# Row lists, expert rows, attention's weight pieces and gate weights' sums of a retention, mixture-of-experts and SoLU kernel at other places of its program

## The chip, the cores and the metric

The kernel runs on one core of a Trainium2 chip. The metric is the device time of one execution in microseconds (us). Before the change it is 546.37 us, the median of 3 runs (546.04 to 546.61).

## The reference

Three layers follow one another. The first is a retention (a linear attention with decay) over 2 batches of 768 steps, 8 heads of 64; its output is 1536 tokens of 512 values. The second gives each token to the best two of 8 experts; the gate has added noise. The third is a dense layer with a softmax-weighted activation and a norm.

```
for t in range(S):                                   # retention
    state = gamma * state + einsum('bhd,bhe->bhde', k[:, :, t], v[:, :, t])
    y[:, :, t] = scale * einsum('bhd,bhde->bhe', q[:, :, t], state)

noisy = x @ w_gate + log1p(exp(x @ w_noise)) * noise # experts
top2 = argpartition(-noisy, 2, axis=1)[:, :2]        # softmax of the two gives top2_w
for e in range(8):
    h = maximum(x[mask] @ w1[e], 0)                  # 512 -> 1024
    out[mask] += top2_w[mask, k] * (h @ w2[e])       # 1024 -> 512

h = x @ w_in                                         # 512 -> 1024
solu = h * softmax(h)
out = (layernorm(solu) * g_ln) @ w_out               # 1024 -> 512
```

## The kernel before

**Order.** Nothing reorders the program. Each engine runs its instructions in the order in which the code issues them, and an instruction that has to wait holds up all behind it on its engine or queue. So the order of the Python code is the order of every engine, and generators (`choose`, `slots`, `load_xg`, `convert_steps`) are stepped with `next` where a piece of their work is to stand. Loads and stores are issued by SP (a few by ACT at the start); gathers by index are issued by POOL, as are the first four weight pieces of the second expert.

**Numbers.** A product of float32 values is made of three: each operand is split into a high part (ACT copies it to a rounded type) and a low part (DVE subtracts). So `hidden` issues 12 matmuls for one block of 128 hidden columns, as xh·wh, xh·wl and xl·wh. The names: `wr` a raw piece of weights (512 KB), `wh` and `wl` its parts, `xh` and `xl` those of an expert's input rows, `hh` and `hl` those of the hidden values.

**Attention.** The loop `for i in range(NT)` runs over 12 tiles of 128 tokens. Of a tile PE makes `y_out` (from state and masked scores), `kv` (the state), `scores` of the next tile, and `x_rows` (rows of x and gate logits in one). DVE makes `vp` (for the first five tiles; ACT later), `pm` (masked scores), `xT` and the logits. Beside this stand the gate's steps: `choose(g)` finds the best two experts for a group of tiles, `rank(g)` each token's place in its expert's list, `slots` and `add_table` turn places into a table of token numbers, `by_rows` spreads the table (`spread`). `feed(split_to, load_to, later)` loads raw weight pieces and splits them; here piece i is split at tile i and three more are loaded.

**First expert.** The expert with most tokens has number 0 in w1 and w2 and is done first, in two parts: `hidden(0, f, slice(0, EARLY))` for 192 rows of the first 8 tiles (f from 0 to 7), then the other 256 rows once their list is there: `rank(3)`, `first_rows(3)`, `list_part(1)`, the gather of the rows, and `first_xt(1)`, which transposes them on PE. `turns` sorts the other experts by their number of tokens.

**The seven others.** `lists` makes `rows_r`, the row numbers for all of them. `load_xg(e)` gathers an expert's rows (four tiles by POOL). For expert 1, PE transposes these (`xg_t`, line 995). From expert 2 on they take another path: stored to `xs` in DRAM, read back as `xq` with the columns regrouped, and transposed by DVE in blocks of 32 (line 999). `load_xg` stops after each gather, each pair of stores and each pair of reads. Before the change it is stepped for expert e + 2 within expert e: gathers at f = 4 to 7 (a POOL copy to `pace` holds each back until `hh` of that f is there), stores in the second half, and the reads at f = 1 and 3 of expert e + 1.

An expert e has 8 blocks of `hidden`, in PSUM banks `b` and `a` in turn (two of each), then `second`: four quarters of 24 matmuls into banks `c0` to `c3` (line 1036). `xg_t` of the next expert stands behind the first two quarters. `y_t` transposes the result of the expert before and stores it to `yg`. `advance` calls `feed` and so sets when pieces are split and loaded: a load waits for one of four buffers, which a split sets free. `convert` makes float32 of the last layer's weights, a piece at a time.

**Last layer.** `weights` makes the two gate weights of each token and the rows of `yg` where its two results lie (`slot_y`). The last expert's second product has three blocks of 128 rows (line 1139); behind the first, POOL starts to gather results (`gather`, line 798), `mix` adds a token's two results, `x2_t` transposes, `h_in` multiplies by w_in (line 837), `solu` and `z_turn` make z and turn it by way of DRAM (`zd`, `zc`), `z_parts` splits it, `out_mm` multiplies by w_out (line 924).

Of the kernel before, what the change touches and what calls it, by code (L numbers as in the profile page):

```python
# [44 lines left out]
def retnet_moe_solu(ctx, tc, qT, kT, k, v, w_gate, w_noise, noise, w1, w2, w_in, w_out, g_ln,  # L45
# [442 lines left out]
    def choose(g):  # L488
# [10 lines left out]
        nc.scalar.activation(r, p[:, :, E:2 * E], AF.Relu)  # L499
        V.scalar_tensor_tensor(ab, th, -1.0, th, op0=OP.mult, op1=OP.max)  # L500
        V.tensor_scalar_mul(nl, ab, LOG2[0])
        for n, c in enumerate(LOG2[1:-1]):
            if n == 0:
                yield
            V.scalar_tensor_tensor(nl, nl, c, ab, op0=OP.add, op1=OP.mult)
# [77 lines left out]
    def add_table(lo):  # L583
        oh, nm = HOT.pop(lo)
        last = oh.shape[1] - 1
        p = bank("a", (128, 32))
# [37 lines left out]
    def first_xt(part, d):  # L624

        n = BLKS[2 * part][1]
        p = bank("a", (128, 2, 2 * n)) if n <= 128 else None
# [11 lines left out]
    def turns():  # L639

        V = nc.vector
        p = bank("c2", (128, E))
# [19 lines left out]
    def lists():  # L662

        p = bank("a", (128, E - 1, 4))
# [30 lines left out]
    def hidden(e, f, c):  # L695
# [7 lines left out]
        for n, (w, x, d) in enumerate(terms):  # L703
            nc.tensor.matmul(p, w[:, 0, f * 128:(f + 1) * 128], x[:, d, c],  # L704
                             start=(n == 0), stop=(n == len(terms) - 1))
        nc.scalar.activation(hh[:, f, c], p, AF.Relu)  # L706
# [20 lines left out]
    for i in range(NT):  # L727
# [5 lines left out]
        if i in (4, 8, 10):  # L733
            next(picks)
        if i == 6:
            next(todo, None)
        if i:
            kv(i)
        if i == 5:
            rank(0)  # L740
        if i == 7:
# [5 lines left out]
        if i == NT - 1:  # L747
            rank(2)
            for d in (0, 2):
                first_xt(0, d)  # L750
# [3 lines left out]
        if i in (5, 9):  # L754
            next(picks, None)
        if i == 5:
# [11 lines left out]
        scale_v(i + 2)  # L768
        if i == 9:
            list_part(0, range(4, 8), "a", last=True)  # L770
        if i in (3, 7, 9, 11):
# [3 lines left out]
            next(picks)  # L775
        if i % 2 == 0:
            dec_t(i // 2 + 1)
        feed(min(i, LEAD), min(i + 3, LEAD + 3), later)
# [4 lines left out]
    next(last_picks, None)  # L783
# [152 lines left out]
    hidden_of(0)  # L936
    for f in range(KF):
# [110 lines left out]
    for e in range(E - 1):  # L1048
        if e:
            hidden_of(e)  # L1050
        for j in range(4):
            for f in (2 * j, 2 * j + 1):
# [22 lines left out]
                if f in (1, 3, 4, 5):  # L1075
                    d = (1, 3, 4, 5).index(f)
                    if e:
                        y_t(e - 1, d)
# [255 lines left out]
```

## Time and profile before

| | us |
|---|---|
| median of 3 runs | 546.37 |
| the profiled execution | 547.89 |
| its span, from the first instruction to the last | 545.8 |
| PE busy (matmuls) | 515.7, 94% |
| DVE busy | 369.6, 68% |
| ACT busy | 232.6, 43% |
| POOL busy | 100.1, 18% |
| TensorE's mean granted clock | 0.981 |

PE, DVE, ACT and POOL are TensorE, VectorE, ScalarE and GpSimd; PEld is TensorE's weight load. A busy time is the sum of an engine's own intervals. The profiled execution lies 2.09 us over its span and 1.52 us over the median. The attention takes the first 76 us of the span, the first expert until 135, the others until 402, the last layer the rest.

In the timeline view a row has the start in us, the length in us, the engine, the line, the operation, written and read tiles, shapes, the number of merged instructions, and in brackets the idle time before with what ended it.

### The profile page before, as it was taken

To read this page: it belongs to the slowest core of one execution; us is meant where nothing else is said; L and a number is where in the kernel's file an instruction comes from. 1 tells how busy PE (TensorE), PEld (TensorE's weight loads), DVE (VectorE), ACT (ScalarE), POOL (GpSimd) and SP (SyncE) were. 2 spreads that over 40 slices of the span, in tenths; PEclk is the share of its full clock that TensorE was granted. 3 is DMA by queue.
4 is the path that set the end of the run, shared out by engine and by line. 5 is a ranking of instruction groups with operands and counts; after the bars stand their busy time and mean duration, and the time that the engine had idled before them with its cause. 6 is when DMAs were issued, how large, how long until landed. Compare 5 with 4: busy or idle time off the path is not lost.

```text
span 545.8 us, 8617 instructions
## 1 busy us (share of the span) xinstructions
PE 515.7 (94%) x3059; PEld 469.8 (86%) x3059; DVE 369.6 (68%) x743; ACT 232.6 (43%) x434; POOL 100.1 (18%) x202
## 2 busy tenths in 40 slices
PE   9889988969999899999999979999989999999996
PEld 8878887859999799999999979999768888888886
DVE  5678778728747877857877658867357676676650
ACT  3576732424423343434425234445345445434341
POOL 4000011250020050220310400000333544331110
PEclk9999999979999899999999997999989999999999
DMA  8998431566694897796996986867453565564341
GB/s 247 344 364 309 136 108 40 171 216 222 195 300 159 276 287 266 215 319 193 296 339 199 242 269 217 216 215 171 140 197 90 159 189 175 158 164 139 96 117 44
DMA packets 71857, 111.92 MB, mean 205 GB/s; under 512 B 9760, under 2 KB 37152, under 8 KB 71808
## 3 DMA queue, kind: packets, MB, share of 16 engines
q1 hardware_dynamic: 65520, 94.58, 57.2%
q0 software_dynamic: 4944, 16.39, 9.5%
q8 instruction: 26, 0.43, 0.3%
q10 hardware_dynamic: 1344, 0.34, 0.3%
q14 instruction: 23, 0.19, 0.1%
HBM read 83.50 MB, written 27.79 MB: 204 GB/s over the span
## 4 chain that ended last, share of the span: by engine, by line
PE 41%; DVE 22%; DMA 15%; ACT 6%; issue 5%; SPq 3%; POOL 0%; DVEq 0%; POOLq 0%; ACTq 0%
PE d L837 12%; PE b L924 12%; DVE wl L195 5%; PE a L704 4%; PE c L1036 4%; PE b L704 4%; DMA yg<-yr 3%; DVE xt L999 3%; DMA xs<-xr 3%; ACT xh L1001 2%; DMA wr<-in_moe_w_dram 2%; DVE hl L707 2%; DMA xq<-xs 2%; DVE xl L1002 2%; ACT wh L194 2%
## 5 line engine op out<-in xcount | busy, mean ns | idle before, releaser
L195 DVE TENSOR_TENSOR wl<-wr,wh 128x1024 fp32r<-128x1024 f32 x68 | 81.4, 1219 | 24.1 <-ACT wh L194 24.1
L1036 PE MATMUL c<-hh,wh 128*128 128x448 f32 (+5 forms) x224 | 80.0, 357 | 0.1
L1036 PE MATMUL c<-hl,wh 128*128 128x448 f32 (+5 forms) x224 | 79.6, 355 | 0.0
L1036 PE MATMUL c<-hh,wl 128*128 128x448 f32 (+5 forms) x224 | 79.4, 355 | 0.0
L194 ACT ACTIVATE wh<-wr 128x1024 fp32r<-128x1024 f32 x68 | 69.6, 1050 | 21.3 <-DMA wr<-in_moe_w_dram 21.3
L704 PE MATMUL b<-xh,wh 128*128 128x192 f32 (+8 forms) x144 | 48.1, 342 | 6.4 <-ACT xh L1001 3.4
L704 PE MATMUL b<-xh,wl 128*128 128x192 f32 (+8 forms) x144 | 47.4, 337 | 0.0
L704 PE MATMUL a<-xh,wh 128*128 128x256 f32 (+7 forms) x128 | 44.1, 348 | 1.4 <-DVE table L589 1.3
L1036 PEld LDWEIGHTS c<-hh,wh 128*128 128x128 f32 x224 | 42.7, 191 | 2.0 <-issue 0.7
L704 PE MATMUL a<-xh,wl 128*128 128x256 f32 (+7 forms) x128 | 43.8, 346 | 0.0
L1036 PEld LDWEIGHTS c<-hh,wl 128*128 128x128 f32 x224 | 42.7, 190 | 1.3
L1036 PEld LDWEIGHTS c<-hl,wh 128*128 128x128 f32 x224 | 42.7, 191 | 1.2
L798 POOL DMA_INDIRECT y<-yg,slot_y x24 | 24.7, 1031 | 90.5 <-DMA yg<-y 77.0
L1073 POOL COPY pace<-hh 1x1 f32<-1x1 f32 x20 | 10.0, 498 | 159.0 <-ACT hh L706 158.8
L837 PE MATMUL d<-wh,x2h 128*128 128x512 f32 x96 | 38.9, 405 | 0.0
L924 PE MATMUL b<-wh,zh 128*128 128x512 f32 (+1 forms) x104 | 38.3, 375 | 0.0
L924 PE MATMUL b<-wl,zh 128*128 128x512 f32 (+1 forms) x104 | 38.2, 374 | 0.0
L837 PE MATMUL d<-wl,x2h 128*128 128x512 f32 x96 | 37.9, 395 | 0.0
L1001 ACT ACTIVATE xh<-xt 128x428 fp32r<-128x428 f32 (+5 forms) x24 | 13.0, 540 | 58.3 <-DVE xt L999 58.3
L837 PE MATMUL d<-wh,x2l 128*128 128x512 f32 x96 | 37.8, 394 | 0.0
L120 ACT ACTIVATE ce<-ce,rebias 128x512 int32<-128x512 int32 x16 | 11.6, 723 | 59.7 <-DVE ce L119 59.7
L704 PEld LDWEIGHTS b<-xh,wh 128*128 128x128 f32 x144 | 27.5, 191 | 8.5 <-ACT xh L1001 4.0
(238 smaller groups left out, 1088.5 us busy)
## 6 DMA issues: line engine op xcount, KB each, us to landing
wr<-in_moe_w_dram SPq DMA_DIRECT2D x60, 512.0 KB, 6.3
zd<-zs SPq DMA_DIRECT2D x40, 128.0 KB, 2.3
zc<-zd SPq DMA_DIRECT2D x10, 512.0 KB, 4.1
xs<-xr SPq DMA_DIRECT2D x18, 256.0 KB, 5.7
raw<-in_moe_w_in_dram SPq DMA_DIRECT2D x8, 512.0 KB, 5.1
raw<-in_moe_w_out_dram SPq DMA_DIRECT2D x8, 512.0 KB, 5.2
xq<-xs SPq DMA_DIRECT2D x16, 208.0 KB, 6.4
yg<-yr SPq DMA_DIRECT2D x16, 208.0 KB, 6.1
```

The costliest lines, as they stand in the source:

```text
L120: nc.scalar.activation(e, e, AF.Relu, bias=rebias, scale=8.0)
L194: nc.scalar.activation(hi, t, AF.Copy)
L195: low = lambda: nc.vector.tensor_sub(lo, t, hi)
L704: nc.tensor.matmul(p, w[:, 0, f * 128:(f + 1) * 128], x[:, d, c], start=(n == 0), stop=(n == len(terms) - 1))
L707: nc.vector.scalar_tensor_tensor(hl[:, f, c], p, 0.0, hh[:, f, c], op0=OP.max, op1=OP.subtract)
L798: nc.gpsimd.indirect_dma_start(out=t, out_offset=None, in_=yg[:upto], in_offset=bass.IndirectOffsetOnAxis(ap=slot_y[:, i, s:s + 1], axis=0))
L837: nc.tensor.matmul(PH[i][:, s, :], x[:, c], w[:, 0, f], start=(n == 0), stop=(n == 3 * KD - 1))
L924: nc.tensor.matmul(p, z[:, f * 128:(f + 1) * 128], unit_t[8 * E + 4 + f // 2][n][:, f % 2, c], start=(m == 0), stop=(m == len(terms) - 1))
L999: nc.vector.transpose(t[:, :32 * n], xr_t[e][:, :n, d:128:KD])
L1001: nc.scalar.activation(hi, t, AF.Copy)
L1002: nc.vector.tensor_sub(lo, t, hi)
L1036: nc.tensor.matmul(py[d][:, :CAPS[e]], c, h[:, f, :CAPS[e]], start=(f == 0 and n == 0), stop=(f == KF - 1 and n == 2))
```

## The change

What moves, by part of the program:

- **Attention.** `feed` splits piece i - 2 at tile i and loads up to i, where it split i and loaded to i + 3. All DVE steps of `choose` stand behind its first stop; the steps of group 0 stand a tile later, those of group 2 half a tile later, so that the masked scores are issued ahead of the long steps of groups 0 and 2. `rank(0)`, `slots(0, 4)` and its table follow a tile later. ACT's `vp` and the splits stand behind `choose`. The first expert's first rows are transposed in banks `c0` and `c1`, ahead of `rank(2)`.
- **First expert.** `rank(3)` and `first_rows(3)` stand ahead of the eviction of block f = 2. `list_part(1)` stands a block sooner (f = 3), the sort of `turns` uses bank `c3`. In the second part the tables stand at f = 3 in banks `c2` and `c3`, the row lists at f = 5 in `c2`; these took banks `a` at f = 4 and 6. PE's transposes of expert 1 stand behind quarters 1 and 2 of `second`, not 0 and 1. `y_bank` takes its four banks at f = 6 and 7.
- **Experts 1 to 5.** Gathers for expert e + 2 at f = 0 to 3, stores at f = 5 and 7, reads in the second half of the same expert (quarters 1 and 2). Expert 2's own reads stay at f = 1 and 3 of expert 1.
- **Last layer.** `weights` moves from expert 1 to the last expert, f = 5. The last two pieces of w_out are loaded behind the third store of results, and split behind `mix(3)`.

The diff, cut to this:

```diff
@@ choose
         nc.scalar.activation(r, p[:, :, E:2 * E], AF.Relu)
+        yield
         V.scalar_tensor_tensor(ab, th, -1.0, th, op0=OP.mult, op1=OP.max)
         V.tensor_scalar_mul(nl, ab, LOG2[0])
         for n, c in enumerate(LOG2[1:-1]):
-            if n == 0:
-                yield
@@ add_table, first_xt: bank("a", ...) -> bank(tag, ...); turns: "c2" -> "c3"; lists: "a" -> "c2"
@@ hidden
+        if between:
+            between()
         nc.scalar.activation(hh[:, f, c], p, AF.Relu)
@@ attention, for i in range(NT)
-        if i in (4, 8, 10):
+        if i in (5, 8, 11):
             next(picks)
-        if i == 6:
+        if i == 7:
             next(todo, None)
-        if i == 5:
-            rank(0)
-        if i == 7:
+        if i == 8:
             add_table(0)
             by_rows()
         if i == NT - 1:
+            for d in (0, 2):
+                first_xt(0, d, f"c{d // 2}")
             rank(2)
-            for d in (0, 2):
-                first_xt(0, d)
-        if i in (5, 9):
+        if i == 9:
             next(picks, None)
-        if i == 5:
+        if i == 6:
             guard(FRONT_TILES)
         x_rows(i)
-        scale_v(i + 2)
+        if i == 5:
+            rank(0)
+            next(picks, None)
             next(picks)
+        scale_v(i + 2)
-        feed(min(i, LEAD), min(i + 3, LEAD + 3), later)
+        feed(min(max(i - 2, 0), LEAD), min(i, LEAD + 3), later)
@@ first expert, early part
     for f in range(KF):
-        hidden(0, f, slice(0, EARLY))
-        if f == 2:
-            rank(3)
-            first_rows(3)
+        hidden(0, f, slice(0, EARLY), newest if f == 2 else None)
         if f == 3:
+            list_part(1, range(4, 12), "c2", last=True)
+            next(last_picks, None)
         if f == 4:
-            list_part(1, range(4, 12), "c2", last=True)
             turns()
@@ for e in range(E - 1)
-                if not e and f == 4:
-                    add_table(4)
-                    add_table(10)
+                if not e and f == 3:
+                    add_table(4, "c2")
+                    add_table(10, "c3")
                     by_rows()
-                if not e and f == 6:
+                if not e and f == 5:
                     lists()
-                if e and f in (1, 3):
+                if e == 1 and f in (1, 3):
                     next(rows, None)
-                if e and e + 2 < E and f > 3:
-                    fresh = fresh if f > 4 else load_xg(e + 2)
+                if e and e + 2 < E and f < 4:
+                    fresh = fresh if f else load_xg(e + 2)
                     nc.gpsimd.tensor_copy(pace, H_t[e][0][:1, f, :1])
                     next(fresh)
+                if e and f in (5, 7):
+                    next(fresh, None)
             second(e, j, py)
-            for d in ((0, 1), (2, 3), (), ())[j]:
+            for d in ((0, 1), (2, 3), (), ())[j] if e else ((), (0, 1), (2, 3), ())[j]:
                 xg_t(e + 1, d)
-            if e == 1 and j == 1:
-                weights()
@@ last expert
+            if f == 5:
+                weights()
         if b == 1:
             y_rows(b, py)
-            feed(n_units - 2, n_units)
             mix(0)
     y_rows(2, py)
+    feed(n_units - 2, n_units)
-    feed(n_units, n_units)
     gather(3)
     mix(3)
+    feed(n_units, n_units)
     h_in(1, 1)
```

DVE in the second part of the first expert, before (`table` and `spread` the token table and its spread form, `rows_r` the row lists, `hl` the low part of a hidden block):

```order
L707 SCALAR_TENSOR_TENSOR hl<-b,hh 128x256
L589 TENSOR_TENSOR table<-table,a 128x32 x2
L596 TENSOR_TENSOR spread<-part,table 128x128
L707 SCALAR_TENSOR_TENSOR hl<-a,hh 128x256
L195 TENSOR_TENSOR wl<-wr,wh 128x1024
L707 SCALAR_TENSOR_TENSOR hl<-b,hh 128x256
L667 TENSOR_SCALAR rows_r<-a 128x28
```

and after:

```order
L588 TENSOR_TENSOR table<-table,c_1510 128x32
L588 TENSOR_TENSOR table<-table,c_1524 128x32
L595 TENSOR_TENSOR spread<-part,table 128x128
L195 TENSOR_TENSOR wl<-wr,wh 128x1024
L708 SCALAR_TENSOR_TENSOR hl<-b,hh 128x256
L708 SCALAR_TENSOR_TENSOR hl<-a,hh 128x256
L666 TENSOR_SCALAR rows_r<-c_1577 128x28
```

Tables and lists each stand a block sooner, and the tables are read from banks of their own.

SP in expert 2 before, from its first reads of `xq` (for expert 3) to its first stores of `xs` (for expert 4):

```order
L982 DMA xq<-xs 32x13x128 x2
L176 ISA
L176 DMA wr<-in_moe_w_dram 128x1024
L176 ISA
L176 DMA wr<-in_moe_w_dram 128x1024
L982 DMA xq<-xs 32x13x128 x2
L176 ISA
L176 DMA wr<-in_moe_w_dram 128x1024
L1023 DMA yg<-yr 32x14x128 x4
```

and after, the same expert from its stores for expert 4 to the first pair of reads for it:

```order
L978 DMA xs<-xr 128x512 x2
L1026 DMA yg<-yr 32x14x128 x4
L176 ISA
L176 DMA wr<-in_moe_w_dram 128x2x512
L125 DMA w_in_70<-co 128x512
L102 DMA raw<-in_moe_w_in_dram 128x512
L978 DMA xs<-xr 128x512
L978 DMA xs<-xr 32x512
```

The stores that stood in the second half now stand among the stores of results and the pieces of weights of the first half; the reads left that place.

POOL in the first expert, before:

```order
L176 DMA wr<-in_moe_w_dram 128x1024
L176 ISA
L176 DMA wr<-in_moe_w_dram 128x1024
L965 DMA xr<-xd,rows_r 128x512 x4
L176 ISA
L176 DMA wr<-in_moe_w_dram 128x1024
```

and after:

```order
L176 DMA wr<-in_moe_w_dram 128x1024
L964 DMA xr<-xd,rows_r 128x512 x4
L176 ISA
L176 DMA wr<-in_moe_w_dram 128x1024
L176 ISA
L176 DMA wr<-in_moe_w_dram 128x1024
```

The four gathers for expert 1 stand ahead of one more piece of its weights.

## Rows read from the trace of the kernel before

**Rows 1.** PE's waits: engine, line, releaser: us in total, times, longest.
```profile
PE a L995 <- DMA xr<-xd,rows_r: 4.7, 3, 2.7
PE b L704 <- ACT xh L1001: 3.4, 2, 2.0
PE a L818 <- DVE t L809: 3.1, 1, 3.1
PE b L704 <- DVE hl L707: 2.7, 2, 2.2
```

**Rows 2.** Stretches of low clock: from:to, length, busy times, PE clock, DMA share, GB/s.
```profile
115.11:121.92 6.81, 5.24 (x17) 4.77 (x18) 2.61 (x5) 2.33 (x4) 2.83 (x3) 0.50 0.82 306
186.79:190.19 3.40, 3.40 (x11) 3.18 (x10) 3.32 (x6) 0.00 (x0) 0.00 (x0) 0.50 0.86 334
326.74:333.55 6.81, 6.21 (x19) 6.22 (x20) 4.43 (x8) 3.23 (x5) 0.00 (x0) 0.50 0.49 119
398.42:401.82 3.40, 3.40 (x11) 2.82 (x11) 1.44 (x2) 1.32 (x2) 0.00 (x0) 0.50 0.79 310
```

**Rows 3.** Timeline of PE in tiles 3 and 4 of the attention.
```profile
26.34 1.16 PE L426 MATMUL s<-qt,kt 64*128 64x128 f32 x16 [1.41 <-DMA qt<-in_qT_dram]
28.33 0.73 PE L476 MATMUL c<-unit,xT 128*128 128x144 f32 x4 [0.83 <-DVE xT L446]
...
34.79 0.73 PE L476 MATMUL c<-unit,xT 128*128 128x144 f32 x4 [1.15 <-DVE rt L505]
```

**Rows 4.** Timeline of DVE in tiles 3 and 4 of the attention.
```profile
26.89 0.69 DVE L413 TENSOR_TENSOR vp<-vt,dec 128x512 f32<-128x512 f32 x1 [3.06 <-DMA vt<-in_v_dram]
...
36.77 1.28 DVE L430 TENSOR_TENSOR pm<-s,causal 128x512 f32<-128x512 f32 x2
```

**Rows 5.** Busy times (PE, PEld, DVE, ACT, POOL) in the first expert's hidden blocks.
```profile
76.11:106.16 30.05, 26.12 (x242) 25.00 (x241) 22.96 (x89) 10.15 (x24) 3.05 (x4) 1.00 0.37 115
```

**Rows 6.** Timeline of PE at block f = 5 of the first expert's second part.
```profile
101.53 0.38 PE L704 MATMUL a<-xh,wh 128*128 128x256 f32 x1 [1.27 <-DVE table L589]
```

**Rows 7.** Chain that ended last, first expert: start, us, what.
```profile
95.54 1.44 PE b L704 x12
...
106.32 4.86 PE c L1036 x24
111.36 5.27 DMA xr<-xd,rows_r
```

**Rows 8.** Timeline of DVE and of POOL at the second gather for expert 1.
```profile
107.72 1.22 DVE L195 TENSOR_TENSOR wl<-wr,wh 128x1024 fp32r<-128x1024 f32 x1 [0.52 <-ACT wh L194]
...
107.88 1.92 POOL L965 DMA_INDIRECT xr<-xd,rows_r  x1 [0.30 <-issue]
```

**Rows 9.** Timeline of DVE in expert 1's second product.
```profile
162.05 0.97 DVE L999 STREAM_TRANSPOSE xt<-xq 128x448 f32<-128x448 f32 x1 [2.84 <-DMA yg<-yr]
...
173.29 0.18 DVE L672 TENSOR_TENSOR tw<-top 128x12 f32<-128x12 f32 x1
...
177.09 0.68 DVE L123 SCALAR_TENSOR_TENSOR ce<-raw,ce 128x512 int32<-128x512 int32 x1
```

**Rows 10.** Timeline of SP and of DVE in expert 5.
```profile
302.89 2.41 SPq L982 DMA_DIRECT2D xq<-xs  x2
...
317.06 0.92 DVE L999 STREAM_TRANSPOSE xt<-xq 128x416 f32<-128x416 f32 x1 [3.42 <-DMA wr<-in_moe_w_dram]
```

**Rows 11.** Chain that ended last, where experts end and in the last layer.
```profile
391.62 5.73 DMA y<-yg,slot_y
...
432.30 5.50 PE b L924 x24
```

**Rows 12.** Timeline of DVE and of ACT in the last layer.
```profile
403.14 2.74 DVE L191 SCALAR_TENSOR_TENSOR wl<-wr,gcol,wh 128x512 fp32r<-128x512 f32 x4 [1.35 <-ACT wh L190]
...
430.24 1.06 ACT L913 ACTIVATE zh<-zc 128x1024 fp32r<-128x1024 f32 x1 [3.05 <-DMA zc<-zd]
```

**Rows 13.** DMA issues from 404 to 413 us: count, median us to landing.
```profile
y<-yg,slot_y POOLq DMA_INDIRECT x6, 3.8
```

More of the change, by code (lines that the diff above doesn't have):

```diff
@@ L581, in slots, with add_table @@
         V.tensor_tensor(oh, col128[:, None, :].to_broadcast(m), pos.to_broadcast(m), op=OP.is_equal)
-    def add_table(lo):
+    def add_table(lo, tag="a"):
         oh, nm = HOT.pop(lo)
         last = oh.shape[1] - 1
-        p = bank("a", (128, 32))
+        p = bank(tag, (128, 32))
         for n in range(last + 1):
@@ L622, in list_part, with first_xt @@
             x0[2 * half + b] = t
-    def first_xt(part, d):
+    def first_xt(part, d, tag="a"):
         n = BLKS[2 * part][1]
-        p = bank("a", (128, 2, 2 * n)) if n <= 128 else None
+        p = bank(tag, (128, 2, 2 * n)) if n <= 128 else None
         for s in range(2):
@@ L641, in turns @@
         V = nc.vector
-        p = bank("c2", (128, E))
+        p = bank("c3", (128, E))
         nc.tensor.matmul(p, ones, cum[:, NT], start=True, stop=True)
@@ L662, in lists @@
     def lists():
-        p = bank("a", (128, E - 1, 4))
+        p = bank("c2", (128, E - 1, 4))
         nc.tensor.matmul(p, spread.rearrange("p a i -> p (a i)"), sort.rearrange("p e s -> p (e s)"),
@@ L693, in retnet_moe_solu, with hidden @@
     place = const.tile([128, NT, 2], F32, name="place")
-    def hidden(e, f, c):
+    def hidden(e, f, c, between=None):
         xh, xl = xgT[e]
@@ L782, in retnet_moe_solu @@
     guard(EARLY_TILES)
-    next(last_picks, None)
     att.close()
@@ L936, in retnet_moe_solu, with newest @@
     hidden_of(0)
+    def newest():
+        rank(3)
+        first_rows(3)
     for f in range(KF):
-        hidden(0, f, slice(0, EARLY))
-        if f == 2:
-            rank(3)
-            first_rows(3)
+        hidden(0, f, slice(0, EARLY), newest if f == 2 else None)
         if f == 3:
+            list_part(1, range(4, 12), "c2", last=True)
+            next(last_picks, None)
             todo = slots(4, 10)
@@ L1068, in retnet_moe_solu @@
                     gx["pool"] = gx_ctx.enter_context(tc.tile_pool(name="gx", bufs=1, side="right"))
-                if e and f in (1, 3):
+                if e == 1 and f in (1, 3):
                     next(rows, None)
-                if e and e + 2 < E and f > 3:
-                    fresh = fresh if f > 4 else load_xg(e + 2)
+                if e and e + 2 < E and f < 4:
+                    fresh = fresh if f else load_xg(e + 2)
                     nc.gpsimd.tensor_copy(pace, H_t[e][0][:1, f, :1])
                     next(fresh)
-                if f in (1, 3, 4, 5):
+                if e and f in (5, 7):
+                    next(fresh, None)
+                if e and f in (1, 3, 4, 5):
                     d = (1, 3, 4, 5).index(f)
-                    if e:
-                        y_t(e - 1, d)
+                    y_t(e - 1, d)
                     y_bank(e, d)
@@ L1081, in retnet_moe_solu @@
                     convert()
+                elif not e and f > 5:
+                    for d in ((0, 1), (2, 3))[f - 6]:
+                        y_bank(e, d)
             advance(e, j)
@@ L1097, in retnet_moe_solu @@
                     next(fresh)
+                rows = fresh
             elif j in (1, 2):
                 next(fresh, None)
-        rows = fresh
     for _ in conv:
```

## The prediction

> **What bounds the kernel now.** I read the table of busy times first: PE has matmuls in flight for 515.7 of 545.8 us. So the time is PE's work plus PE's waits, and the other engines count only where PE waits for them. The waits of PE come next [rows 1]: four places make up 13.4 us or more. They are the start of expert 1 (4.7, three waits for gathered rows), the start of expert 6 (3.4), the first transpose of the last layer (3.1) and expert 2 (one wait of 2.2 in the fourth row). Then the clock by stretches [rows 2]. Behind each of these four waits the granted clock falls to one half, 1.2 of 2.4 GHz, and is back at full level some microseconds later. PE was busy 5.24, 3.40, 6.21 and 3.40 us in these stretches; at full clock that work takes half the time, so the falls cost 2.6, 1.7, 3.1 and 1.7. With its fall, each wait is worth: 7.3 at expert 1, 3.9 at expert 2, 6.5 at expert 6, 4.8 in the last layer. Last I read the timeline of the attention and of the first expert, where the waits are shorter and the clock stays full.
>
> The Trainium skill, page "TensorE: Matmul & The Clock Gate", section "HAM oscillation — how this bites in real kernels", takes the penalty as the throttled time times the missing half of the clock: half of 20.42 us here [rows 2], 10.2 us. The rows give 9.1, since PE still stood idle for a part of two stretches; by the page the sum below would be up to 1.1 larger.
>
> **The change part by part**, as gains in us.
>
> *Attention: 2.5.* Tile 3 waits 1.41 for q and 0.83 for xT, whose DVE queue stood 3.06 behind v [rows 3, 4]. Three weight pieces issued at tile 0 lie ahead of these loads in the same queue. After the change the first piece follows tile 1, so these 2.24 go. The other half is order on DVE. In tile 4 the steps of `choose` stood ahead of xT and of pm: PE waits 1.15 [rows 3], and pm starts at 36.77 [rows 4] though its scores were done some 3 us before. Behind the change pm goes first. But the work does not get less: the four low parts of weights (1.22 each [rows 8]) now fall on tiles 4 to 7, together with all steps of groups 0 and 1, and a tile has about 5.3 us on PE. I laid tiles 4 to 11 out on DVE with the durations of the timeline and got about as much new waiting (tiles 5, 8 and 9, and `rank(2)`, which stands behind the late xT of the last tile) as goes. So the reordering is put at 0.3, and its ends are -2.5 (all of it a new queue) and +3.5 (none of the new waits).
>
> *First expert until its second part: 1.3.* The list a block sooner and its bank for `turns` remove waits for the list, the gather and a bank. PE stands idle 30.05 - 26.12 = 3.9 in this stretch [rows 5], of which 1.27 is the next term; 2.6 are left. But DVE is busy 22.96 of 30.05, and nearly without a break until the last rows are split; that split ends ahead of PE's need no more once the gather comes sooner. So DVE is next late, and I take half, 1.3, with ends 0 and 2.6.
>
> *Tables with their own banks: 1.3.* Block f = 5 waited 1.27 for bank `a`, which DVE's table addition held [rows 6]. Banks `c2` and `c3` are idle there. Ends 0 and 1.3.
>
> *Rows of expert 1: 6.6 of 7.3.* Count from the block that starts at 95.54, called E [rows 7]. The last gather issued at 111.36 = E + 15.8 and landed 5.27 later, E + 21.1; the transposes stood behind the first quarter, at 106.32 + 4.86 = E + 15.6. So rows were 5.4 late (of which the first tile's transposes used a little). After the change the lists' product has one block less (1.44 [rows 7]) and no wait (1.27) ahead, some 2.6 sooner with rounding: last landing E + 18.5. The second product starts 1.27 sooner and the transposes stand a quarter later: E + 15.6 - 1.3 + 4.9 = E + 19.2. That leaves 0.7 of slack, with the long landing of 5.27; so the wait and the fall of the clock go. POOL now issues three pieces of expert 1's weights behind the gathers, which are split ahead of the first transposed rows on ACT and DVE, which hold the two `a` banks of the second transposes. I put 0.7 of a new wait there; ends 0 and 4.7 (below).
>
> *Gate weights' sums and expert 2: 3.9.* `weights` held DVE from 173.29 to 177.09, 3.8 [rows 9], ahead of the evictions that PE waited 2.2 for [rows 1]. It leaves that queue. Besides, DVE waited 2.84 for `xq` at 162.05 [rows 9]; the reads stay where they are in the code, but their stores come sooner, since DVE and ACT no longer stand behind the transposes of expert 1 (the splits go ahead and free the buffers for which SP waited). Both together are 6.6 against 2.2. In its new place `weights` meets an ACT queue that waits for DVE's first subtraction (0.2) and a DVE queue with the last hidden blocks behind it; their low parts are needed some 8 us later at the end of the next product's first block. Ends: 2.2 and 3.9.
>
> *Reads of `xq` an expert sooner: 6.5.* DVE waited until 317.06 for rows read at 302.89 [rows 10], and PE 3.4 for DVE. Now the reads stand in the second half of the expert before, some 20 us ahead of need. What is late next is DVE itself, which finished these splits in the other experts in time. The stores at f = 5 stand ahead of the stores of results and of a weight piece on SP, and wait there for gathers of f = 0 and 1: four blocks of 2.4 (half of 4.86 [rows 7]) lie between, about 10 us. I see no wait of PE in it. Ends: 3.4 and 6.5.
>
> *Last layer: 0.1.* The second gather took 5.73 [rows 11] beside two weight pieces; these move behind, and six such gathers without them took 3.8 [rows 13]. But DVE splits 3.8 later the piece whose buffer the last w_out load of this stretch needs, and ACT copies that load ahead of the first results: I put 0.7 later there. So the wait of 3.1 becomes 1.9, nearest to that of 2.2, behind which the clock fell: the fall stays. Gain 1.2. Then the last two pieces' low parts (2.74 [rows 12]) now stand ahead of z's chain on DVE, where 0.6 was idle: z, its turn through DRAM and `zh` are 2.1 later. `zh` was ready at 431.3 [rows 12], PE's product near 432.2 [rows 11]: 0.9 of slack, so 1.1 of new wait. Sum 0.1; ends -1.5 and 3.7.
>
> **Sum:** 2.5 + 1.3 + 1.3 + 6.6 + 3.9 + 6.5 + 0.1 = 22.2. Against the profiled execution, 547.9 - 22.2 = 525.7; against the median, which is 1.5 below it, 546.4 - 22.2 = **524.2 us**.
>
> **The rivals.**
>
> *POOL's queue holds expert 1 back.* A gather normally takes some 1.25 there; one took 1.92 + 0.30, beside a DVE subtraction [rows 8]. The three weight pieces follow from about E + 15; with a landing of more than 6 us they are split after E + 24, the first transposed rows after that, and PE, due at E + 24.9 for the second ones, waits. At 3 us the clock falls again, 1.7 more: 528.2. For it: the slack is under 1 us. Against: in the forecast DVE and ACT are free from E + 10 on. The Trainium skill, page "SBUF — State Buffer", section "SBUF: two separate sides", says that POOL cannot write its descriptors while DVE holds the port pair that they share. The one long gather [rows 8] agrees; the chance of this rival is put for that reason at the upper end.
>
> *DVE bounds the attention*: the new order gives back what the loads bring (-2.5 in the first term): 526.7. For it: tiles 4 to 8 hold more DVE work than PE work. Against: pm goes first.
>
> *A clean last layer*: the first wait there gets so short that the clock stays (1.7) and z's chain is not late (1.1): 521.4. It takes a load of w_out that is not delayed.
>
> *The boundaries do not clear*: the reads, now beside the next expert's weight pieces, make those late instead, and waits like those of experts 2 and 6 come back (10.4): 534.6. Against: the second half has the quieter transfers.
>
> *Slower than before: SP.* In experts 1 to 5, SP stands at the new stores until the gathers land, and all weight pieces behind it are late. If each of the five loses 3.1 and a fall of 1.7, that is 24.0 against the 22.2 of the sum and 548.2 in all. The point is a landing of over some 10 us for the gathers of f = 1, in every expert, with no lead of weights left; the one in [rows 7] took 5.27.
>
> **How the numbers follow.** Forecast (522 to 526) 0.55; clean last layer 0.15; POOL's queue 0.13; DVE in the attention 0.08; boundaries 0.05; SP 0.04. From 518.5 to 530 lie the forecast with the bounds of its terms (mostly -2.5 to +3.5 of the attention, 0 to 2.6 of the first expert) and the three rivals nearest, and somewhat over 0.8 of the chance remains when their own spread is taken off. A measurement of this kernel can tell about 0.2%, 1.1 us. Only SP's rival is slower: 0.04; no case lies within 0.2%, and I leave 0.01 for it; 0.95 faster.
>
> **What would show it.** Right: no wait of PE at line 995's transposes and no half clock near 115, 187 and 327; `xt` never waiting for `xq` from expert 3 on; PE's first hidden block of the first expert near 73.5 us, where it was 76.1; the two `table` additions without a PE wait; one shorter wait at the first transpose of the last layer, and a new one of about 1 us at the second product with w_out. Wrong: ACT waiting long for weight pieces in experts 1 to 5, a wait at the second transposes of expert 1, or xT late in several tiles of the attention.

## Result and profile after

The changed kernel takes 528.0 us (median of 4 runs, 527.31 to 529.43) beside 546.2 for the kernel before (4 runs, 541.75 to 546.61): a ratio of 0.9688, 95% interval 0.9633 to 0.9743. The forecast of 524.2 was 3.8 too low; the time lies in the range of 518.5 to 530.0. The profiled execution took 527.31, with a span of 525.3; PE has matmuls in flight for 508.4 of it, and its mean granted clock is 0.991.

PE's waits, the answer to [rows 1] (engine, tile, line, releaser: us in total, times, longest):

```profile
PE b L703 <- DVE hl L708: 2.7, 1, 2.7
PE a L819 <- DVE t L810: 2.7, 1, 2.7
PE c L476 <- DVE xT L446: 1.4, 2, 1.0
...
PE c L629 <- DMA xr<-xd,rows: 0.7, 1, 0.7
PE b L703 <- DVE xl L634: 0.7, 1, 0.7
...
PE b L925 <- ACT zh L914: 0.5, 1, 0.5
```

No wait for gathered rows of expert 1 is left in the list, none at expert 2 and none at expert 6. The wait of the last layer is there (3.1 before). The first line is new: it stands in expert 5, where the kernel before had none.

The two stretches of low clock and five stages by windows, the answer to [rows 2] (from:to, length, busy us of PE, PEld, DVE, ACT and POOL, PE clock, DMA share, GB/s). The windows are, in order: the two stretches, the first expert's hidden blocks (as [rows 5]), its second product, expert 2, expert 5, expert 6.

```profile
280.72:284.13 3.41, 3.41 (x12) 3.40 (x11) 3.41 (x5) 1.70 (x4) 3.24 (x4) 0.50 1.17 179
376.29:379.71 3.42, 3.42 (x10) 2.86 (x11) 1.36 (x2) 1.21 (x2) 0.06 (x1) 0.50 0.46 144
...
71.56:98.88 27.32, 26.17 (x242) 25.06 (x241) 22.98 (x91) 10.28 (x25) 3.87 (x5) 1.00 0.34 107
98.88:120.18 21.30, 21.30 (x114) 19.72 (x113) 13.01 (x19) 10.00 (x14) 8.73 (x10) 1.00 0.88 294
159.10:196.21 37.11, 37.11 (x193) 36.19 (x192) 29.12 (x46) 13.82 (x21) 7.28 (x8) 1.00 1.01 298
267.41:307.24 39.83, 36.69 (x193) 36.01 (x193) 31.81 (x51) 16.80 (x25) 5.99 (x7) 0.96 0.85 241
307.24:341.70 34.46, 34.19 (x194) 33.81 (x193) 26.82 (x44) 15.47 (x23) 0.00 (x0) 1.00 0.77 212
```

Two stretches at half clock are left of four, 1.7 us each (half of PE's 3.4). In the second product of the first expert PE is busy for the whole window, 21.30 of 21.30; before, this stage took 29.04.

The stages of both kernels, each from the start of its first matmul on PE to that of the next stage (us):

| stage | before | after | gain | forecast |
|---|---|---|---|---|
| attention | 76.11 | 71.56 | 4.55 | 2.5 |
| first expert, hidden | 30.05 | 27.32 | 2.73 | 2.6 |
| first expert, second product | 29.04 | 21.30 | 7.74 | 6.6 |
| expert 1 | 38.91 | 38.92 | 0.0 | |
| expert 2 | 41.65 | 37.11 | 4.54 | 3.9 |
| experts 3 and 4 | 71.85 | 71.20 | 0.65 | |
| expert 5 | 34.86 | 39.83 | -4.97 | |
| expert 6 | 40.86 | 34.46 | 6.40 | 6.5 |
| expert 7 to the first h_in | 38.28 | 38.02 | 0.26 | 1.2 |
| first h_in to the third out_mm | 42.04 | 43.47 | -1.43 | -1.1 |
| rest of the last layer | 97.83 | 97.83 | 0 | |
| sum | 541.48 | 521.02 | 20.46 | 22.2 |

So the terms of the forecast sum up to 1.7 less than forecast. The other 2.1 of the miss come from which executions were profiled: that of before lay 1.5 above the median from which the forecast was made, that of after 0.7 below its own (the profiled times differ by 20.6).

That the time still lies in the range is in part luck: what expert 5 loses (4.97) is nearly made up by terms that were put too low, 2.05 in the attention, 1.14 in the first expert's second product, 0.64 at expert 2, and by 0.65 at experts 3 and 4, for which the forecast had nothing.

### The profile page after: what moved, and what is told of

It reads as the page before. It is cut to its first block, busy times and chain, and to the rows that moved or that the text cites. A ratio compares the mean times of both kernels' runs of the same rounds, so it can differ in the third digit from the quotient of the medians.

```text
span 525.3 us, 8618 instructions
## 1 busy us (share of the span) xinstructions
PE 508.4 (97%) x3059; PEld 464.2 (88%) x3059; DVE 369.2 (70%) x743; ACT 231.3 (44%) x434; POOL 100.8 (19%) x202
## 4 chain that ended last, share of the span: by engine, by line
PE 57%; DVE 18%; DMA 12%; issue 5%; ACT 4%; SPq 2%; DVEq 0%; ACTq 0%
PE c L1039 14%; PE b L925 12%; PE d L838 9%; PE b L703 7%; PE a L703 7%; DMA wr<-in_moe_w_dram 4%; DVE wl L195 4%; DMA yg<-yr 2%; DMA xr<-xd,rows_r 2%; PE c L443 1%; PE s L426 1%; ACT wh L194 1%; DVE xt L1002 1%; DVE hl L708 1%; PE c L454 1%
## 5 line engine op out<-in xcount | busy, mean ns | idle before, releaser
L194 ACT ACTIVATE wh<-wr 128x1024 fp32r<-128x1024 f32 x68 | 70.1, 1051 | 31.4 <-DMA wr<-in_moe_w_dram 31.2
L1076 POOL COPY pace<-hh 1x1 f32<-1x1 f32 x20 | 8.2, 411 | 135.7 <-ACT hh L707 135.6
L968 POOL DMA_INDIRECT xr<-xd,rows_r x27 | 31.3, 1159 | 15.2 <-DMA xs<-xr 5.2
```

What stands on the lines that cost most here:

```text
L194: nc.scalar.activation(hi, t, AF.Copy)
L968: nc.gpsimd.indirect_dma_start(out=t[b], out_offset=None, in_=xd[:], in_offset=bass.IndirectOffsetOnAxis(ap=rows_r[:, e - 1, b:b + 1], axi ...
```

## Experiments

Each changes one thing in the kernel that is named; ratios are to the kernel before, run beside it. Between these rounds the kernel before itself moved (medians of 543.3 to 546.5), so two edited kernels are compared by their ratios or by stages of their profiled executions. The stages are read as in the table.

**The rows' transfers back to their old place.**

```diff
-                if e == 1 and f in (1, 3):
+                if e and f in (1, 3):
                     next(rows, None)
-                if e and e + 2 < E and f < 4:
-                    fresh = fresh if f else load_xg(e + 2)
+                if e and e + 2 < E and f > 3:
+                    fresh = fresh if f > 4 else load_xg(e + 2)
...
-                if e and f in (5, 7):
-                    next(fresh, None)
...
-                rows = fresh
             elif j in (1, 2):
                 next(fresh, None)
+        rows = fresh
```

> The changed kernel with one part undone: from expert 1 on, the gathers for expert e + 2 stand at f = 4 to 7 again, their stores in the second half of e and the reads of xq at f = 1 and 3 of expert e + 1. In the changed kernel PE gained 6.4 us at expert 6 and lost 5.0 us at expert 5, where DVE's first low parts of hidden values came late. Theory A, the moved transfers made both: the wait at expert 5 (2.7, with a fall of the clock) goes, the one at expert 6 (3.4, with a fall) is back, and the time is 528.0 + 6.4 - 5.0 = 529.4. Theory B, the wait at expert 5 comes from weight pieces that run short, since all experts before have become quicker by 19 us at the same bytes: it stays, there or at a neighbour, beside the one at expert 6, and the time is 528.0 + 6.4 = 534.4.

529.37 us (526.37 to 530.44), ratio 0.9692. Expert 5 is free of the wait (18.01 for its hidden blocks, 22.55 in the changed kernel), and PE waits at expert 6 again, four times (the fourth is 0.44), and once at expert 4 (0.95):

```profile
306.94 0.44 PE L703 MATMUL b<-xh,wh 128*128 128x388 f32 x1 [0.75 <-ACT xh L1004]
308.91 0.44 PE L703 MATMUL b<-xh,wh 128*128 128x388 f32 x1 [1.35 <-ACT xh L1004]
...
318.14 0.44 PE L703 MATMUL b<-xh,wh 128*128 128x388 f32 x1 [1.54 <-DVE hl L708]
```

Theory A holds: the part that frees expert 6 also makes the wait at expert 5. Its net gain, 1.4 by the medians, is not clear of the spread: the ratios are 0.9692 without and 0.9688 with it.

**The same part alone, in the kernel before.** The same lines, the other way round.

> The kernel before with one part of the change alone: gathers, stores and reads of the experts' rows an expert sooner, as in the changed kernel. Theory A: the late reads on SP make the wait at expert 5 by themselves: PE's waits at expert 6 (3.4) go, one of some 2.7 at expert 5 comes, and the time changes by less than 1.5 us. Theory B: the wait at expert 5 needs the experts before it to be quicker as well, since then weight pieces run short; with the waits of experts 1 and 2 still there, they have 10 us more: expert 6 is freed, nothing comes at expert 5, and the time is 5 to 6.5 us shorter.

544.88 us (540.07 to 546.74), ratio 0.9977 (0.9944 to 1.0009). Expert 6 takes 33.9 us, 7 less, and expert 5 has a new wait and a half clock behind it:

```profile
298.12 0.70 PE L704 MATMUL b<-xh,wh 128*128 128x396 f32 x1 [2.52 <-DVE hl L707]
...
297.68:301.08 3.40, 2.96 (x9) 2.96 (x10) 3.32 (x6) 2.84 (x5) 2.71 (x4) 0.50 0.99 236
```

So the wait at expert 5 does not need the experts ahead of it to be quicker: theory A again. The part moved a wait from expert 6 to expert 5. By the stages of these two executions 3.1 us are left of it (6.9 gained, 3.8 lost); in the time that is not shown, as the interval of the ratio holds 1.

**Where the wait at expert 5 comes from.** SP in expert 3's second product and at expert 4's start, in the changed kernel (start, us, queue, line, written and read, issues):

```profile
223.32 2.88 SPq L176 DMA_DIRECT2D wr<-in_moe_w_dram  x2
232.31 0.35 SPq L125 DMA_DIRECT2D w_out<-co  x1
232.72 0.42 SPq L102 DMA_DIRECT2D raw<-in_moe_w_out_dram  x1
233.41 0.39 SPq L176 DMA_DIRECT2D wr<-in_moe_w_dram  x1
234.24 0.84 SPq L985 DMA_DIRECT2D xq<-xs  x2
235.88 0.37 SPq L176 DMA_DIRECT2D wr<-in_moe_w_dram  x1
236.29 1.67 SPq L985 DMA_DIRECT2D xq<-xs  x2
```

From 226.2 to 232.3 SP issues nothing: it stands at the store of a converted piece, which needs DVE's `co`. The reads of `xq` are behind it, though the stores of their rows went at 221. The transfers show it (windows from 226.00 to 232.20 and on to 254.20; the last two numbers are DMA share and GB/s):

```profile
226.00:232.20 6.20, 6.20 (x35) 6.20 (x34) 4.95 (x7) 2.04 (x3) 0.00 (x0) 1.00 0.40 147
232.20:254.20 22.00, 22.00 (x121) 21.73 (x120) 15.43 (x28) 7.84 (x13) 6.13 (x8) 1.00 1.02 261
```

Six quiet microseconds, then 22 full ones, in which the four reads, four gathers, five pieces of weights and the converted pieces fall together. ACT waits for a piece there, in expert 4's second product, and from then on DVE is late until expert 5's first `hl`:

```profile
254.20 1.06 ACT L194 ACTIVATE wh<-wr 128x1024 fp32r<-128x1024 f32 x1 [5.63 <-DMA wr<-in_moe_w_dram]
...
279.66 0.45 PE L703 MATMUL b<-xh,wh 128*128 128x396 f32 x1 [2.73 <-DVE hl L708]
```

How long the pieces took is seen in the kernel with the last w_out pieces back (below), which has the same order here: transfers issued from 232.3 to 245 us (count, KB each, median us to landing), and the one piece issued just ahead of the quiet stretch:

```profile
wr<-in_moe_w_dram SPq DMA_DIRECT2D x5, 512.0 KB, 13.0
xq<-xs SPq DMA_DIRECT2D x4, 208.0 KB, 10.5
...
wr<-in_moe_w_dram SPq DMA_DIRECT2D x1, 512.0 KB, 4.6
```

**The reads ahead of the pieces on SP**, on top of the kernel with the last w_out pieces back, in two forms.

```diff
+            if e and j in (1, 2):
+                next(fresh, None)
             advance(e, 4 + j)
...
-            elif j in (1, 2):
-                next(fresh, None)
```

In the second form the first two lines read `if e and j == 1:` and step through all that is left of `fresh`.

> The changed kernel with the last two w_out pieces back at their old place and one thing new: in the experts' second products the two reads of xq stand ahead of the pieces of weights and the store of a converted piece on SP, not behind them. In the traces with the late reads, these are issued at 232 to 237 us, after a time of 6 us in which nothing is in flight and SP stands at the store of a converted piece; the burst behind it makes a weight piece of expert 4 take 13.9 us, and DVE is late at expert 5. Theory A (the burst makes the wait at expert 5): the reads go at 227 to 229, the pieces land 2 to 3 us sooner, the wait of 2.74 falls to under 1 and its clock fall goes: 524.5 - 4 = 520.5. Theory B (the pieces run short for want of transfers in all): the wait stays or moves, 524.5. Theory C: SP now waits at the reads for the stores of xs, and weight pieces behind it are later: above 525.

521.26 us (520.75 to 522.44), ratio 0.9608 (0.9573 to 0.9643).

> As the kernel before in this list, with all four reads of xq ahead of the pieces at the second quarter, not two there and two at the third. Theory A: as there or up to 0.5 better, since all four go before the burst: 520 to 520.5. Theory B: 524.5. Theory C, four reads that wait for the stores of xs in one place hold SP longer: 525 and more.

521.09 us (519.54 to 521.83), ratio 0.9602 (0.9568 to 0.9636); the two can't be told apart. SP and the windows of the second form:

```profile
221.12 2.99 SPq L176 DMA_DIRECT2D wr<-in_moe_w_dram  x2
225.01 1.88 SPq L985 DMA_DIRECT2D xq<-xs  x4
230.23 0.34 SPq L125 DMA_DIRECT2D w_out<-co  x1
...
225.00:230.20 5.20, 5.20 (x30) 5.20 (x29) 3.95 (x7) 2.03 (x3) 0.00 (x0) 1.00 1.00 231
```

The four reads now fill the stretch that was quiet. Here is what ACT waits for pieces in the whole span, in the changed kernel and in this one (us in total, times, longest):

```profile
ACT wh L194 <- DMA wr<-in_moe_w_dram: 31.2, 13, 5.6
...
ACT wh L194 <- DMA wr<-in_moe_w_dram: 8.8, 6, 3.9
```

PE's waits of this kernel have no line for `hl` any more; one wait longer than 1.2 us is left in the whole span:

```profile
PE a L819 <- DVE t L810: 3.0, 1, 3.0
PE c L266 <- DVE ones L263: 1.2, 1, 1.2
```

The bytes and the work are those of the changed kernel. So pieces do not run short; the order on SP made them late. The rows of `xq` themselves were not what came late: in the changed kernel no transpose of them on DVE has idle time before it that ends with their landing. What the order is worth is seen in the stage: expert 5 takes 34.56 here and 39.27 in the kernel with the w_out pieces back. By the medians it is 3.4 (524.5 to 521.1, and the runs of the two do not overlap), but they ran in different rounds, and the ratios (0.9616 and 0.9602) do not tell them apart. Of all kernels run, these two and one built on them (last below) have the lowest times, 7 us below the changed one by the medians, some half of it from the w_out pieces.

**The last two w_out pieces at their old place.**

```diff
             y_rows(b, py)
+            feed(n_units - 2, n_units)
             mix(0)
     y_rows(2, py)
-    feed(n_units - 2, n_units)
...
+    feed(n_units, n_units)
     gather(3)
...
     mix(3)
-    feed(n_units, n_units)
```

> The changed kernel with one part undone: the last two pieces of w_out are loaded behind the second store of results and split ahead of the first product with w_in, as before. Theory A (the prediction's): their low parts of 2.7 us stand ahead of z's chain, which makes the waits of 0.53 and 0.21 us in the last layer and the idle time around them; undone, PE needs 1.5 us less from the first product with w_in on, the first transpose waits 0.3 us more as the gather goes beside the pieces again, and the time is 526.8. Theory B: z's chain is late for another reason (the gathers, which now follow each other differently); then the two small waits stay and the time is 528.0 to 528.4.

524.47 us (523.88 to 524.67), ratio 0.9616 (0.955 to 0.9681): 3.5 quicker than the changed kernel, where theory A said 1.2. From the first h_in to the third out_mm PE needs 41.94, as before the change (42.04; 43.47 in the changed kernel): the 1.5 are shown. The first wait of the last layer is 3.61 here against 2.73, so the later loads did save 0.9 there in this pair; over all traces but that of the last experiment the wait is 2.3 to 2.8 in the six with the later loads, 3.0 to 3.6 in five with the old place and 1.25 in one (the pieces alone, below). But behind the 3.61 the clock stays at full level in this execution, which gives back 1.7; this is the part that theory A did not have. The profiled executions differ by 2.6, 1.5 of it from the first h_in on and 0.7 in the stage ahead of it; the rest lies in stages that this edit does not touch.

**The gate weights' sums back in expert 1.**

```diff
-            if f == 5:
-                weights()
...
+            if e == 1 and j == 1:
+                weights()
             advance(e, 4 + j)
```

> The changed kernel with one part undone: the gate weights' sums stand in expert 1 again, behind the second quarter of its second product, not in the last expert. Theory A (the prediction's): they hold DVE for 3.8 us there, ahead of the low parts of expert 2; a wait at expert 2 comes back, of 1 to 2.2 us and with it a half clock that costs up to 1.7: 529 to 531.9. Theory B: the rows of xq that came late were the cause, and DVE has room now: no wait at expert 2, 528.0.

527.78 us (525.29 to 529.68), ratio 0.9667. In the profile theory A holds, with a longer wait than it said: PE waits 3.37 at expert 2 and the clock is halved behind it; the stage takes 42.68, 5.6 more than in the changed kernel.

```profile
171.95 0.46 PE L703 MATMUL b<-xh,wh 128*128 128x428 f32 x1 [3.37 <-DVE hl L708]
...
173.31:176.72 3.41, 3.41 (x12) 3.14 (x11) 3.38 (x5) 0.02 (x1) 2.65 (x2) 0.50 1.18 204
```

The profiled execution is only 2.0 longer (529.31 beside 527.31): it had no half clock at expert 5 nor in the last layer, where the changed kernel had two, and so it got back 2.3 and 1.6 there. Two of the other runs (526.24 and 525.29) lie below all of the changed kernel. The place of the sums is the cause of the wait at expert 2; what it is worth in the time, these runs cannot tell.

**The transposes of expert 1's rows behind quarters 0 and 1.** The list of the loop is that of the kernel before for all e.

> The changed kernel with one part undone: PE transposes expert 1's rows behind quarters 0 and 1 of the first expert's second product, not 1 and 2; the lists, tables and gathers stay a block sooner. The last gather was issued at 101.0 us and the first quarter ends at 103.8. Theory A (the prediction's): a gather takes some 5 us to land there, so PE waits 2 to 3 us behind the first quarter and the clock falls to one half behind it: 2 to 5 us slower, 530 to 533. Theory B: the sooner gathers alone are enough and the later place of the transposes gives nothing: 528.0.

528.13 us (526.91 to 529.85), ratio 0.9679. PE waits once, for a gather:

```profile
PE a L998 <- DMA xr<-xd,rows_r: 2.2, 1, 2.2
```

The stage takes 23.82 against 21.30, and the next two 0.8 and 0.5 more; the clock stays full in this stage. Theory A holds for the wait and not for the fall. Of the 7.74 gained in this stage, the later transposes carry 2.5; the other 5.2 (of it 2.6 for the half clock of [rows 2] at 115) come with the other edits, the sooner lists and gathers among them. In the median it is not seen.

**The attention's halves.** First the pieces at their old tiles:

```diff
-        feed(min(max(i - 2, 0), LEAD), min(i, LEAD + 3), later)
+        feed(min(i, LEAD), min(i + 3, LEAD + 3), later)
```

> The changed kernel with one part undone: in the attention, weight pieces are split at tile i and loaded up to i + 3 again; DVE's order stays as changed. The changed kernel reaches the first expert's first block at 71.56 us, 4.55 before the kernel before; the prediction gave 2.24 of that to the pieces and 0.3 to the order. Theory A (the prediction's): the waits of tile 3 for q and for x come back, the first block starts at 73.5 to 74, and the time is 2 to 2.5 us longer. Theory B, the loads are the whole of it, since DVE and ACT are also rid of splits while they are late: the first block starts at 76, and the time is 4 to 4.5 longer. Theory C, the order is: 72, no difference to be measured.

528.47 us (525.02 to 532.26), ratio 0.9721; the first block starts at 73.23, 1.67 later than in the changed kernel. The waits of tile 3 are back:

```profile
26.37 1.16 PE L426 MATMUL s<-qt,kt 64*128 64x128 f32 x16 [1.56 <-DMA qt<-in_qT_dram]
28.36 0.73 PE L476 MATMUL c<-unit,xT 128*128 128x144 f32 x4 [0.83 <-DVE xT L446]
```

Then the order of DVE as before, the pieces as changed (the positions of `choose`, `rank(0)`, `slots`, the first table and `scale_v` of the diff, the other way round):

> The changed kernel with one part undone: in the attention the steps of the expert choice, the first ranks and the first table stand where they stood, ahead of the masked scores in the tiles 4, 5, 8 and 10; the weight pieces stay late and first_xt stays ahead of the last rank. Theory A (the prediction's): the order carries 0.3; the first block of the first expert starts at 71.9, and the time can't be told from the changed kernel's. Theory B: the order carries what the prediction had too little of, some 2 us: the first block starts at 73.5 to 74 and the time is 2 to 2.5 longer.

525.07 us (524.43 to 528.93), ratio 0.9695; the first block starts at 71.65, 0.1 later. That is nothing that can be told: eight of the profiled kernels, the changed one among them, have the changed attention word for word, and their first blocks start between 71.16 and 72.06.

And the pieces alone, in the kernel before (the line of the first half, the other way round):

> The kernel before with one part of the change alone: in the attention, piece i - 2 is split at tile i and pieces are loaded up to i. Undoing one half of the attention's change costs 1.67 us (the pieces) or 0.1 us (the order) at the first block of the first expert, while both together bring 4.55. Theory A, the two halves remove the same waits, DVE's lateness: the pieces alone bring nearly all, the first block starts at 71.6 to 72.5 where it started at 76.11. Theory B, the rest comes from the other edits there (the banks of first_xt, its place ahead of the last rank): the pieces alone bring 1.7 to 2.3, and the first block starts at 73.8 to 74.4. The waits of the later stages stay as in the kernel before, so its time falls by 4 (A) or 2 (B).

543.37 us (537.41 to 545.72), ratio 0.9954 (0.992 to 0.9988); the first block starts at 72.34. The pieces alone bring 3.77 of 4.55. What is left of PE's waits in the attention then (tiles 4 to 11):

```profile
33.79 1.25 PE L443 MATMUL c<-pm,vp 128*64 128x128 f32 x16 [0.66 <-DVE pm L430]
37.86 0.73 PE L476 MATMUL c<-unit,xT 128*128 128x144 f32 x4 [0.59 <-DVE xT L446]
...
68.44 1.25 PE L443 MATMUL c<-pm,vp 128*64 128x128 f32 x16 [0.53 <-DVE pm L430]
```

Beside [rows 3, 4], tile 3's two waits (2.24) are gone and tile 4's 1.15 too, with the order of DVE untouched: the latter was the tail of tile 3's late queue. On top of that, all the other edits of the attention bring 0.8 (72.34 to 71.56), which is less than that spread of 0.9. The order of `choose` and its followers removes the small waits of these rows and brings others, the 0.96 for xT, 0.67 for `pm` and 0.75 for first rows in the first list of the result. Theory A of the last run holds by the start of the block; the time fell by 0.7 to 4.4 us (the interval of the ratio), which does not tell its 4 from the 2 of theory B. The halves overlap: the pieces bring 3.77 alone, and their undoing costs 1.67 where the order is changed too.

**The first transposes of the last layer three matmuls later**, on top of the second form of the reads.

```diff
-            if b == 2 and f == KF - 2:
+            if b == 2 and f == KF - 1:
                 x2_t(0)
```

> The kernel with all four reads ahead of the pieces (521.1 us, 3.0 us of waiting at the first transposes of the last layer, and a fall of the clock behind it), with those transposes and the second mix behind 21 of the 24 matmuls of the last block, not 18. Theory A: 0.65 us of the wait is covered and comes back behind the transposes, where three matmuls fewer cover the splits; the sum is the same and so is the time, 521. Theory B: the wait in two shorter pieces leaves the clock at full level, and 1.7 us are saved: 519.4.

520.54 us (520.17 to 521.48), ratio 0.9531 beside a kernel before that ran at 545.61 in these rounds. The wait is 3.5, not shorter, and the clock falls behind it as in the kernel without this edit. The stage from expert 7's second product to the first h_in takes 21.56 against 21.52. The gathered results came later in this execution, by 1.2 counted from the second product's start, so whether the wait would split into two stays open; in the time nothing can be told.

## Why the prediction was off by 3.8, point by point

**Reads of xq: the step that failed.** The forecast took 6.5 and the trace has 6.40 at expert 6. But "the stores ... wait there for gathers ... I see no wait of PE in it" looked only at the stores. The reads were taken to stand "in the second half of the expert before, some 20 us ahead of need", where the code has them; on SP they come behind a store that waits for DVE, and go at the next expert's start, beside its gathers and pieces. ACT then waits 5.63 for a piece and PE 2.73 for `hl`, with a half clock behind it. That cost 4.97 at expert 5. The rival named it (the reads "make those late instead") with a chance of 0.05 and the right mechanism; it came at one boundary of five. The order of SP was there to be read: the reads stood behind `advance`, which issues the store of a converted piece, and [rows 9 and 10] show how late DVE runs at the ends of experts.

**Attention: mis-sized.** 4.55 against 2.5. The 2.24 of tile 3 were counted as all that the loads bring, and the waits of tiles 4 and on were given to the order of DVE. Tile 4's 1.15 belonged to the same late queue. The new waits that were feared in tiles 5, 8 and 9 are 0.96 and 0.67, less than what went.

**Expert 1's rows: right, mis-sized by 1.1.** The wait and the fall went; the 0.7 put for the banks did not come, since the transposes in the changed kernel start with no idle time before them. POOL issued the four gathers in 0.95 to 1.47 us each, so the rival of POOL's queue did not come, and that its 528.2 is near the measured 528.0 is chance. Long gathers as in [rows 8] do exist: the traces before and after have eight of 1.78 to 1.99, each beside at least 0.9 us of a DVE subtraction of two tiles; none of them is one of these four.

**Expert 2: right.** 4.54 against 3.9, and the sums put back bring the wait back by themselves; the sooner stores of `xq` did not prevent it.

**First expert and tables: right.** 2.73 against 2.6. The waits for lists, gather, bank and table are gone, and DVE is next late, as forecast: its `xl` by 0.74. How much of the 2.6 of waiting DVE would keep was not worked out but taken as half; without the table's 1.27 the gain is 1.46, so the half was a good guess.

**Last layer: right on the new wait, wrong on the gain.** The forecast gave 1.2 at the first wait and 1.1 lost at z. The loss is 1.43: 0.74 of it as waits (0.53 and 0.21), the rest as busy time, for which PE has 42.72 there in place of 42.04 for the same 198 matmuls. The gain is 0.26 (the wait itself is 0.36 shorter). DVE's low parts do stand ahead of z's chain as worked out, from 392.40 until `zl` (the low part of z) starts:

```profile
392.40 2.73 DVE L191 SCALAR_TENSOR_TENSOR wl<-wr,gcol,wh 128x512 fp32r<-128x512 f32 x4
395.05 1.28 DVE L894 TENSOR_TENSOR zl<-a,zh 128x512 fp32r<-128x512 f32 x2
...
411.28 0.51 PE L925 MATMUL b<-wh,zh 128*128 128x512 f32 x1 [0.53 <-ACT zh L914]
```

Before, this stood in a time when DVE waited anyway ([rows 12]). This part of the change costs more than it brings in these traces: its undoing gave 1.5 back from the first h_in on, against a first wait longer by 0.9.

**The clock's falls: a step that was too simple.** Each wait was given its fall as a fixed price. The falls that the forecast counted did go, but whether a wait of this size has one is not fixed (next section but one), and so a sum against one execution can be off by some 1.7 us for each such wait. The three runs shown before lay within 0.6 us; later rounds of the same kernel ran from 541.3 to 548.5.

**Signs.** Those of the three freed waits and of the full clock near 115, 187 and 327 came as written, so did `xt`, which never waits for `xq`, and the small wait at the second out_mm (0.53, for about 1). The first expert starts at 71.56, not 73.5. One sign of being wrong came as well: ACT waits long for weight pieces, 5.63 in expert 4's second product, ahead of the wait at expert 5, and 31.2 in the whole span where it was 21.3.

## What to carry to other kernels

Where a transfer is issued is told by its queue, not by its line in the code: before moving one sooner, list what stands ahead of it on that queue and what each of these waits for. Here four reads moved ahead of one waiting store were worth 4.7 us at expert 5 (39.27 to 34.56) and 3.4 by the medians, and without that the whole move, made alone, could not be told from no change. Waits that follow each other on a late engine are one wait: give the gain to the first of them, and expect two edits that both shorten it not to add up.

## What was not expected of the hardware

Whether the clock falls behind a wait of PE is not told by the wait's length. At expert 5 a wait of 2.73 has a half clock behind it in the changed kernel (the first row of the windows above) and one of 2.75 has none with the old order of the attention; in the last layer 2.73 has one, and 2.62 there (old order of the attention) and 3.61 (old place of w_out) have none. Nor are short waits safe: in the kernel before with the pieces alone, two waits of 0.54 and 0.96 in the first expert have a granted clock of 0.75 behind them (81.6 to 88.4), where the kernel before has 0.47 and 0.96 and a full clock. Windows of the two kernels without the fall, the first two lines with the old order of the attention behind its two waits, the third with w_out's old place around its wait:

```profile
279.46:282.86 3.40, 3.40 (x19) 3.40 (x20) 3.32 (x6) 2.41 (x4) 3.13 (x3) 1.00 1.05 204
374.75:378.15 3.40, 3.40 (x17) 2.88 (x18) 1.36 (x2) 1.81 (x3) 0.76 (x1) 1.00 0.52 149
...
373.00:380.00 7.00, 3.39 (x18) 2.67 (x17) 2.12 (x3) 2.71 (x5) 2.51 (x3) 1.00 0.84 317
```

What a fall costs can be read from these pairs. Expert 5's hidden blocks take 22.55 with it and 20.85 without, the stage from expert 7's second product to the first h_in 21.36 and 19.67: 1.7 each time. The Trainium skill, page "TensorE: Matmul & The Clock Gate", section "HAM oscillation — how this bites in real kernels", takes the penalty as the throttled time times the missing half of the clock; with the stretches of 3.41 and 3.42 that is 1.7, and the traces agree. That executions of one kernel differ by some us would fit with falls that come in some and not in others. The mean granted clock of every run is on record, and it bears that out only in part: over 33 runs of the kernel before, the time falls as the clock rises (correlation -0.46), but eight of them with the same mean clock, 0.984, take 543.4 to 548.5. So falls of the clock are at most a part of the spread, and the cause of the rest stays open.
